# Matmuls of zeros in TensorE's idle time of the early plan, and accumulators at fixed places in PSUM, in an mLSTM layer followed by an ELU feed-forward

## The chip, the cores and the metric

One core of a Trainium2 chip. The metric is the device time of one execution in microseconds. TensorE (PE) has a clock with two levels, 1.2 and 2.4 GHz; the profile gives the granted level of a stretch as 0.50 or 1.00.

## The reference

For 4 batches, 8 heads, 768 steps and a head size of 40, a matrix memory is decayed, updated and read at every step; the result is gated, and the 3072 rows of 320 go through two weight matrices with an ELU between them, all in float32:

```python
m_new = max(f + m, i);  fs = exp(f + m - m_new);  is_ = exp(i - m_new)
C = fs * C + is_ * outer(v, k);   n = fs * n + is_ * k
y = sigmoid(o) * (C @ q) / max(|n . q|, 1)
h = x @ w_in                      # x: y as (3072, 320); w_in (320, 2048)
g = where(h > 0, h, exp(min(h, 0)) - 1)
out = g @ w_out                   # w_out (2048, 320)
```

## The kernel before

The sequence is cut into 6 chunks of 128 steps; with 4 batches that makes 24 tiles. `gate_chunk(c)` prepares the gates of a chunk: scans on VectorE (DVE), exponentials on ScalarE (ACT), and one TensorE transpose (line 467) whose result `iT` every tile of the chunk needs. `attention(n)` makes one tile: `products` (L555, scores of 8 heads), `values` (L563, `va`, from `iT`), `spread` (L581, TensorE copies a row of gates to all partitions; only in the first two chunks), `decays` (L595, a VectorE scan over it), the product of scores and decays (L609), `outputs` (L623 and L631), `update` (L644) and `gather` (a copy or an addition into `C`), `denominators` (L673), `result` (L687, `xf`), and `turn` (L704), three transposes; ScalarE (L707) and VectorE (L710) split the result into two float32r parts, `xh` and `xl`.

`conversion(i)` (L324 to L358) splits a piece of the weights into two float32r parts. It passes through ScalarE, VectorE, GpSimd (POOL), ScalarE and VectorE again. `ffn` runs over units: a unit is a block of 2 or 3 tiles and a range of the 16 slices of the hidden layer. For each slice there are 8 matmuls into `h` (L746), two ScalarE activations (L754, L757), a VectorE operation (L759), the split into `gh` (ScalarE, L762) and `gl` (L764), and 3 matmuls for each tile of the block into the tile's accumulator (L773). At the end of a unit each accumulator is copied to SBUF, by whichever of ScalarE and VectorE the plan picks (L232), or added to an earlier sum (L791), and stored.

The order is made by `Plan`: each operation is recorded with a cost for each engine that may run it, and `run` plays them against those costs, giving each free engine the ready operation of the best rank. Pools have a number of buffers (`room`); an operation waits until a buffer is free. The order that results is fixed for each engine, and engines execute it in order. Semaphores, and so waits, come from the tile framework, by which tile an instruction touches. Before, each accumulator is a tile of its own, `T("acc", (u, j), P, 512)`, from a pool of three in PSUM; for each of them the next user waits for the last reader.

Of the kernel before, what the change touches and what calls it, by code (L numbers as in the profile page):

```python
# [11 lines left out]
F32 = mybir.dt.float32  # L12
F32R = mybir.dt.float32r
BF16 = mybir.dt.bfloat16
# [6 lines left out]
P = 128  # L21
# [16 lines left out]
class Plan:  # L38
# [38 lines left out]
        self.ops.append(o)  # L77
        return o

    def run(self):  # L80
        for i, o in enumerate(self.ops):
            o.number = i
        for o in reversed(self.ops):
            own = min(o.engines.values())
            if o.nbytes:
                own += self.LAND + o.nbytes / self.RATE
            o.tail = own + max([0.0] + [a.tail for a in o.after if a.rank == o.rank])
        users = {}
        for o in self.ops:
            for k in o.touched:  # L90
                if k[0] in self.room:
                    users[k] = users.get(k, 0) + 1
        taken = {p: [] for p in self.room}
        given, free_at = set(), {}
        waits = {o: len(o.before) for o in self.ops}
        when = {o: 0.0 for o in self.ops}
        pending = [o for o in self.ops if not waits[o]]
        engines = {e: 0.0 for o in self.ops for e in o.engines}
        queue, port, t, order, events = 0.0, 0.0, 0.0, [], {0.0}

        def fits(o):
            new = {}
            for k in o.touched:
                if k[0] in self.room and k not in given:
                    new[k[0]] = new.get(k[0], 0) + 1
            for k in o.touched:
                if k[0] in self.in_turn and k not in given and k[1] != len(taken[k[0]]):
                    return False
            for p, count in new.items():
                for i in range(count):  # L110
                    j = len(taken[p]) + i - self.room[p]
                    if j >= 0 and free_at.get(taken[p][j] if j < len(taken[p]) else None, 1e9) > t:
                        return False
            return True

        while len(order) < len(self.ops):
            assert events, "nothing can go on"
            t = min(events)
            events.discard(t)
            again = True  # L120
            while again:
                again = False
                ready = sorted(
                    (o for o in pending if when[o] <= t), key=lambda o: (o.rank, -o.tail, o.number)
                )
                ahead = dict.fromkeys(engines, 0.0)
                ahead["port"] = 0.0

                def start(o, e):

                    x = max(engines[e], t) + ahead[e]
                    return max(x, max(port, t) + ahead["port"]) if e in o.port else x

                for o in ready:
                    if not fits(o):
                        continue
                    best = min(o.engines, key=lambda e: start(o, e) + o.engines[e])
                    if start(o, best) > t:
                        ahead[best] += o.engines[best]
                        if best in o.port:  # L140
                            ahead["port"] += o.engines[best]
                        continue

                    for k in sorted(o.touched, key=str):
                        if k[0] in self.room and k not in given:
                            given.add(k)
                            taken[k[0]].append(k)
                    end = t + o.engines[best]
                    engines[best] = end
                    if best in o.port:  # L150
                        port = end
                    events.add(end)
                    if o.nbytes:
                        queue = max(queue, end, self.BEGIN) + o.nbytes / self.RATE
                        end = queue + self.LAND
                        engines[best] = max(engines[best], queue - self.DEEP)
                        events.add(engines[best])
                    order.append((t, o.number, best, o))
                    pending.remove(o)
                    for a in o.after:  # L160
                        waits[a] -= 1
                        hop = 0.0 if best in a.engines and len(a.engines) == 1 else self.HOP
                        when[a] = max(when[a], end + hop)
                        if not waits[a]:
                            pending.append(a)
                            events.add(when[a])
                    for k in o.touched:
                        if k in users:
                            users[k] -= 1
                            free_at[k] = 1e9  # L170
                            self.last[k] = max(self.last.get(k, 0.0), end + self.HOP)
                            if not users[k]:
                                free_at[k] = self.last[k]
                                events.add(free_at[k])
                    again = True
                    break
        self.end = max(engines.values())
        self.order = order
        for _, _, e, o in order:
            o.fn(e)  # L180
# [3 lines left out]
def tile_mlstm_then_elu_ffn(  # L184
# [11 lines left out]
    nc = tc.nc  # L196
    PSUM = bass.MemoryType.PSUM
    B, NC, _, D, _, HH, L = qk.shape
    DM, DFF = w_in.shape[1], w_in.shape[0] * w_in.shape[2]
# [9 lines left out]
    SPLITS = [(0, 8), (1, 8), (2, 8), (0, 16)]  # L209
    W2N = 2  # L210

    SPREAD_BY_PE = 2
    TMAX = max(BLOCKS)
    WMAX = max(512, W2N * DM)
# [8 lines left out]
    room = dict(  # L223
        wide=3, narrow=2, gates=2, rest=1, qk=3, bb=3, vko=3, w=3, va=2, wl=2, dec=2, den=2, xf=2,
        x=3, ps_a=3, h=2, acc=3, e=2, gh=4, gl=4, os=3,
    )
    plan = Plan(room, ("qk", "bb", "e", "gh", "gl", "os"))
    op = plan.op
    eng = {"PE": nc.tensor, "DVE": nc.vector, "ACT": nc.scalar, "POOL": nc.gpsimd, "SP": nc.sync}

# [13 lines left out]
    const = ctx.enter_context(tc.tile_pool(name="const", bufs=1))  # L244
    pools = {}

    def pool(name, space=None):
        kw = dict(space=space) if space is not None else {}
        pools[name] = ctx.enter_context(tc.tile_pool(name=name, bufs=room[name], **kw))
# [5 lines left out]
    pools["rest"] = ctx.enter_context(tc.tile_pool(name="rest", bufs=1))  # L255
    pool("ps_a", PSUM)
    pool("h", PSUM)
    pool("acc", PSUM)
    tiles = {}

    def T(name, i, *shape, dt=F32, part=""):

        if (name, i, part) not in tiles:
            tiles[name, i, part] = pools[name].tile(list(shape), dt, name=name + part)
        return tiles[name, i, part]
# [13 lines left out]
    conv_of_2 = {}  # L279
    for f in range(NF):  # L280
        g, j = divmod(f, G)
# [432 lines left out]
    def ffn(u, kb, f0, f1):  # L714
        tl = blocks[kb]
        nt = len(tl)
# [4 lines left out]
            return T("x", kb, P, 3, TMAX * L, dt=F32R, part=part)[:, t, 0:N]  # L721

        def acc(j):
            return T("acc", (u, j), P, 512)[:, 0:DM]

        for f in range(f0, f1):
            g, j = divmod(f, G)
            fs = slice(j * P, (j + 1) * P)
            k = step[u, f]
# [38 lines left out]
            def second_layer(e, f=f, g=g, j=j, ff=ff):  # L768
# [7 lines left out]
                        )  # L776

            op({"PE": 3 * nt * 0.147}, second_layer,
               (KG, KL, ("conv", conv_of_2[f // W2N], 0)), tuple(("acc", (u, a)) for a in range(nt)) + (("turn", 2),))
        for a, n in enumerate(tl):  # L780
            c, b = divmod(n, B)

            def os(a=a):
                return T("os", osn[u, a], P, DM)

            KA, KOS = ("acc", (u, a)), ("os", osn[u, a])
            if f0 > 0:
                op({"SP": 0.06}, lambda e, os=os, n=n: nc.sync.dma_start(os(), sums[n]),
                   (("sum", n),), (KOS,), nbytes=P * DM * 4)
                op(two_ps(DM),  # L790
                   lambda e, os=os, a=a: nc.vector.tensor_add(os(), acc(a), os()),  # L791
                   (KA,), (KOS,))
            else:
                op({"ACT": 0.15 + 0.00088 * DM, "DVE": 0.1 + 0.001 * DM},
                   lambda e, os=os, a=a: copy(e, os(), acc(a)), (KA,), (KOS,))
            if f1 < NF:

                def keep(e, os=os, n=n):
                    sums[n] = dram.tile([P, DM], F32, name=f"sum{n}_{f1}")
                    nc.sync.dma_start(sums[n], os())  # L800

                op({"SP": 0.06}, keep, (KOS,), (("sum", n),), nbytes=P * DM * 4)
            else:
                op({"SP": 0.06},
                   lambda e, os=os, b=b, c=c: nc.sync.dma_start(
                       out[b * S + c * L : b * S + (c + 1) * L, :], os()),
                   (KOS,), (), nbytes=P * DM * 4)
# [16 lines left out]
    step, osn, begin, need = {}, {}, {}, {}  # L824
# [40 lines left out]
        conversion(i)  # L865
    for u, (kb, f0, f1) in enumerate(units):
        ffn(u, kb, f0, f1)
    plan.run()


_OUT = ((3072, 320), "float32")
# [31 lines left out]
```

## Time and profile before

| | |
|---|---|
| median of 3 runs | 495.1 us (493.95 to 495.77) |
| the profiled execution's own time | 494.69 us |
| its span, first to last instruction | 492.6 us |
| busy: PE, DVE, ACT, POOL | 93%, 74%, 59%, 24% |
| chain that ended last, by engine | PE 86%, DVE 11%, ACT 2% |

The span leaves out 2.1 us around the first and the last instruction. A run of matmuls overlaps: the time from one start to the next is shorter than the length of one, so a run of n takes less than n lengths. Rows of TensorE's weight loads (PEld) run beside its matmuls.

### The profile page before, as it was taken

Reading aid. Unit: us, or ns where it says so; the run is one execution under the profiler, and the core shown is the slowest. Engines: PE = TensorE matmul, PEld = TensorE weight load, DVE = VectorE, ACT = ScalarE, POOL = GpSimd, SP = SyncE. Lnnn points to the kernel's source line nnn. Section 1 sums busy time; section 2 is a strip of 40 time slices with the busy share of each in tenths; the row PEclk is TensorE's granted clock in tenths of the full one; section 3 lists DMA queues with packets and bytes.
Section 4 is the critical chain, followed back from the end, with each engine's and each line's share of the span. In section 5 each row is a group of like instructions: output and inputs, shape, how many; then the busy total and the mean of one; then the engine's idle time right before and its main releaser. Section 6 shows DMA issues by size and latency. Waiting matters only on the chain.

```text
span 492.6 us, 12520 instructions
## 1 busy us (share of the span) xinstructions
PE 456.1 (93%) x5006; PEld 432.6 (88%) x5006; DVE 362.2 (74%) x752; ACT 288.4 (59%) x681; POOL 117.6 (24%) x151
## 2 busy tenths in 40 slices
PE   2535889999999999999999999999999999999997
PEld 2334878999999999999989999999999999999996
DVE  8989898998787987965896478873678365546543
ACT  3555945779876564646456464475447544654664
POOL 2444484244231253121220101430012031000000
PEclk9999979999999999999999999999999999999999
DMA  7665544433325353421441034540333030100000
GB/s 266 176 208 166 167 136 138 134 110 127 106 82 154 100 164 110 154 84 42 133 145 43 28 110 127 153 124 1 111 111 109 1 97 1 43 1 1 28 1 27
DMA packets 39001, 49.51 MB, mean 101 GB/s; under 512 B 3072, under 2 KB 31648, under 8 KB 38944
## 3 DMA queue, kind: packets, MB, share of 16 engines
q1 hardware_dynamic: 38944, 48.72, 31.9%
q8 instruction: 39, 0.64, 0.5%
q14 instruction: 18, 0.15, 0.1%
HBM read 43.32 MB, written 5.39 MB: 99 GB/s over the span
## 4 chain that ended last, share of the span: by engine, by line
PE 86%; DVE 11%; ACT 2%; issue 1%; DVEq 0%; ACTq 0%
PE h L746 36%; PE acc L773 34%; PE ps_a L555 5%; PE ps_a L631 3%; PE ps_a L623 3%; DVE w L595 2%; PE ps_a L644 1%; PE ps_a L704 1%; DVE narrow L343 1%; DVE w L358 1%; DVE narrow L333 1%; DVE e L759 1%; DVE narrow L338 1%; PE h L581 1%; DVE w L609 1%
## 5 line engine op out<-in xcount | busy, mean ns | idle before, releaser
L746 PE MATMUL h<-xh,w 128*128 128x384 f32 (+1 forms) x720 | 179.6, 325 | 3.6 <-DVE w L595 2.2
L773 PE MATMUL acc<-w,gh 128*128 128x320 f32 x768 | 175.4, 315 | 1.5 <-DVE w L358 1.5
L773 PEld LDWEIGHTS acc<-w,gh 128*128 128x128 f32 x768 | 128.3, 189 | 3.9 <-DVE w L358 1.7
L746 PEld LDWEIGHTS h<-xh,w 128*128 128x128 f32 x720 | 126.1, 189 | 6.4 <-DVE w L595 2.6
L759 DVE SCALAR_TENSOR_TENSOR e<-e,h 128x384 f32<-128x384 f32 (+1 forms) x144 | 72.7, 505 | 72.6 <-ACT e L757 71.9
L754 ACT ACTIVATE e<-h 128x384 f32<-128x384 f32 (+1 forms) x144 | 65.4, 454 | 101.8 <-PE h L746 96.0
L773 PE MATMUL acc<-w,gl 128*128 128x320 f32 x384 | 119.3, 311 | 0.0
L746 PE MATMUL h<-xl,w 128*128 128x384 f32 (+1 forms) x432 | 113.0, 320 | 0.0
L762 ACT CAST gh<-e 128x384 fp32r<-128x384 f32 (+1 forms) x144 | 67.8, 472 | 34.9 <-DVE e L759 34.8
L764 DVE TENSOR_TENSOR gl<-e,gh 128x384 fp32r<-128x384 f32 (+1 forms) x118 | 64.1, 544 | 27.0 <-ACT gh L762 23.9
L746 PEld LDWEIGHTS h<-xl,w 128*128 128x128 f32 x432 | 77.1, 189 | 0.0
L773 PEld LDWEIGHTS acc<-w,gl 128*128 128x128 f32 x384 | 72.5, 189 | 0.8 <-DVE gl L764 0.6
L757 ACT ACTIVATE e<-e 128x384 f32<-128x384 f32 (+1 forms) x144 | 70.5, 490 | 3.8
L595 DVE TENSOR_TENSOR_SCAN w<-w,ident 128x512 f32<-128x512 f32 x32 | 40.0, 1249 | 5.6 <-DMA w<-f_d 5.4
L764 POOL TENSOR_TENSOR gl<-e,gh 128x384 fp32r<-128x384 f32 (+1 forms) x26 | 25.4, 978 | 63.2 <-ACT gh L762 59.0
L348 POOL TENSOR_TENSOR narrow<-narrow,wide 128x512 int32<-128x512 int32 (+1 forms) x18 | 27.4, 1523 | 41.9 <-DVE narrow L343 24.5
L570 ACT ACTIVATE vko<-vko 128x320 f32<-128x320 f32 x72 | 33.6, 467 | 2.7 <-DMA vko<-in_vko 1.9
L555 PE MATMUL ps_a<-qk 40*128 40x128 f32 x384 | 32.4, 316 | 0.0
L609 DVE TENSOR_TENSOR w<-ps_a,w 128x512 f32<-128x512 f32 x48 | 31.1, 679 | 1.3 <-PE ps_a L555 0.8
L555 PEld LDWEIGHTS ps_a<-qk 40*128 40x128 f32 x384 | 27.4, 216 | 4.4 <-issue 3.7
L655 POOL TENSOR_TENSOR C<-C,dec 40x164 f32<-40x164 f32 x28 | 16.1, 576 | 60.8 <-PE ps_a L623 59.8
L563 POOL TENSOR_TENSOR va<-vko,iT 128x320 f32<-128x320 f32 x15 | 14.1, 938 | 65.6 <-issue 33.4
(87 smaller groups left out, 419.8 us busy)
## 6 DMA issues: line engine op xcount, KB each, us to landing
vko<-in_vko SPq DMA_DIRECT2D x24, 480.0 KB
w<-f_d SPq DMA_DIRECT2D x32, 256.0 KB
qk<-in_qk SPq DMA_DIRECT2D x48, 160.0 KB
wide<-in_w_out SPq DMA_DIRECT2D x8, 640.0 KB
wide<-in_w_in SPq DMA_DIRECT2D x8, 512.0 KB
out<-os SPq DMA_DIRECT2D x24, 160.0 KB
bb<-b_d SPq DMA_DIRECT2D x40, 80.0 KB
sum<-os SPq DMA_DIRECT2D x8, 160.0 KB
```

Source lines behind the costliest of these rows:

```text
L348: lambda e: nc.gpsimd.tensor_add(narrow(), narrow(), words()[0]),
L555: nc.tensor.matmul(ps(two, P, HH, L)[:, j, :], kt[rows, j, :], qt[rows, j, :], start=True, stop=True,)
L570: lambda e, fn=fn, kw=kw: nc.scalar.activation(v3()[2], v3()[2], fn, **kw), (), (KS,))
L595: nc.vector.tensor_tensor_scan(a, f, ident4.rearrange("p h t -> p (h t)"), 0.0, op0=ALU.mult, op1=ALU.add)
L609: lambda e, half=half: nc.vector.tensor_mul(w(half), ps(half, P, HH, L), w(half)),
L746: nc.tensor.matmul(h(), a[g][:, fs], m, start=(i == 0), stop=(i == len(prods) - 1))
L754: op(act(N), lambda e, h=h, ff=ff: nc.scalar.activation(ff("e"), h(), AF.Relu, scale=-1.0), (KHP,), (KE,))
L757: lambda e, ff=ff: nc.scalar.activation(ff("e"), ff("e"), AF.Exp, scale=-1.0), (), (KE,))
L759: lambda e, h=h, ff=ff: nc.vector.scalar_tensor_tensor(out=ff("e"), in0=ff("e"), scalar=-1.0, in1=h(), op0=ALU.add, op1=ALU.max),
L762: op(act(N), lambda e, ff=ff: nc.scalar.copy(ff("gh", F32R), ff("e")), (KE,), (KG,))
L764: lambda e, ff=ff: eng[e].tensor_sub(ff("gl", F32R), ff("e"), ff("gh", F32R).bitcast(F32)),
L773: nc.tensor.matmul(acc(a), x[:, sl], bw[g][:, j, :], start=(f == f0 and i == 0), stop=(f == f1 - 1 and i == 2),)
```

## The change

`run` takes an operation `idle` and a time `until`. Whenever no operation can be started at a moment of the plan, and TensorE is free and the plan's clock is below `until` (60 us), it places one `idle`, `keep_warm`: four matmuls of a 128 by 128 bf16 tile of zeros by itself, planned at 0.24 us, which add zeros to columns 384 to 511 of the first accumulator's bank, which no accumulator uses. Two VectorE memsets ahead of everything else set the tile and these columns to zero. The plan places 163 of them (652 matmuls).

The three accumulators become parts of one tile, `accs`, and are given out in turn: accumulator `osn[u, j]` lies at place `osn[u, j] % 3`, and `acc` joins the list of pools that are taken in a fixed order. The test for that order now lets an operation take several places at once.

```diff
-    def run(self):
+    def run(self, idle=None, until=0.0):
...
-                if k[0] in self.in_turn and k not in given and k[1] != len(taken[k[0]]):
-                    return False
+                if k[0] in self.in_turn and k not in given:
+                    if not 0 <= k[1] - len(taken[k[0]]) < new[k[0]]:
+                        return False
...
+                else:
+                    if idle and engines["PE"] <= t < until:
+                        order.append((t, len(self.ops), "PE", idle))
+                        fillers += 1
+                        engines["PE"] = t + idle.engines["PE"]
+                        events.add(engines["PE"])
...
+    WARM = 60.0
...
-    plan = Plan(room, ("qk", "bb", "e", "gh", "gl", "os"))
+    plan = Plan(room, ("qk", "bb", "e", "gh", "gl", "os", "acc"))
...
-    pool("acc", PSUM)
+    ps_o = ctx.enter_context(tc.tile_pool(name="ps_o", bufs=1, space=PSUM))
+    accs = ps_o.tile([P, room["acc"], 512], F32, name="acc")
...
-            return T("acc", (u, j), P, 512)[:, 0:DM]
+            return accs[:, osn[u, j] % room["acc"], 0:DM]
...
-    plan.run()
+    warm = const.tile([P, P], BF16, name="warm")
+    nc.vector.memset(warm, 0.0)
+    nc.vector.memset(accs[:, 0, 512 - P :], 0.0)
+
+    def keep_warm(e):
+        for _ in range(4):
+            nc.tensor.matmul(
+                accs[:, 0, 512 - P :], warm, warm, start=False, stop=True, skip_group_check=True
+            )
+
+    plan.run(Op({"PE": 0.24}, keep_warm, (), 0, False), WARM)
```

Three places of the order follow (a line of the changed kernel is 12 above its fellow of before from L400 on; names in brackets are the semaphores that an instruction waits for: PE_49 TensorE's, DVE_49 VectorE's, Activation_49 ScalarE's, Pool_49 GpSimd's, DMAHW a transfer's).

The start of TensorE's queue, before, up to the second `spread` matmul:

```order
L897 UNCONDITIONAL_BRANCH [waits barrier_Pool_Activation_PE_DVE_SP_release]
L467 MATMUL ps_a<-ident,gatesi 128x32 [waits Activation_49,Pool_49]
L581 LDWEIGHTS sel [waits DVE_49]
L581 MATMUL h<-fgs,sel 128x128 [waits DVE_49]
L581 LDWEIGHTS sel
```

and with the change, with the pair `LDWEIGHTS warm`, `MATMUL acc<-warm` repeated 143 times where the first line of dots stands (36 fillers) and 11 times where the second does (3 fillers):

```order
L919 UNCONDITIONAL_BRANCH [waits barrier_Pool_Activation_PE_DVE_SP_release]
L886 LDWEIGHTS warm [waits DVE_49]
L886 MATMUL acc<-warm 128x128 [waits DVE_49]
...
L479 MATMUL ps_a<-ident,gatesi 128x32 [waits Activation_49,Pool_49]
L886 LDWEIGHTS warm
L886 MATMUL acc<-warm 128x128
...
```

The transpose of the gates, the first instruction of the queue before, now stands behind 36 fillers. Further on, in the same way: 1, 4, 5 and 13 fillers up to the first `turn`, 8 up to the second tile's `products`, 12, 4 and 2 around the next `spread`s, 32 and 14 before and after the `spread` that ran at 38 us, 1, 1, 1 and 11 up to the first slice of the first layer, 3 behind it, 10 between the third tile's `turn` and the second slice, and 2 ahead of the first second layer. None stands behind that. Apart from the fillers TensorE's order is the same.

VectorE's queue behind the denominators of the first tile (`-` before, `+` with the change; the same instructions on either side of them); the copy of `C` and the small copy of `xf` are now in ScalarE's queue, as is one copy of `wl` further on:

```order
 L232 COPY C_146<-ps_a 40x4x41 x2
 L683 TENSOR_TENSOR vko<-vko,den 128x320
 L687 TENSOR_TENSOR xf<-ps_a,vko 128x320
 L358 TENSOR_TENSOR w_119<-narrow,w_119 128x512
 L232 COPY xf<-xf 128x64
```

That piece is the queue of before; with the change its first and its last row are gone from it and the three between them follow each other.

VectorE's queue at the end of the unit that ends at 425 us in the trace, before; `os_5879` and `os_5883` are the first and the third accumulator's copy, the second's, `os_5881`, is ScalarE's and waits for PE_49 as well:

```order
L764 TENSOR_TENSOR gl_5868<-e_5849,gh_5866 128x256 [waits PE_49,Activation_49]
L232 COPY os_5879<-acc_5307 128x320 [waits DMAHW0_49,PE_49]
L232 COPY os_5883<-acc_5315 128x320 [waits DMAHW2_49,PE_49]
L759 SCALAR_TENSOR_TENSOR e_5896<-e_5896,h_5870 128x256 [waits DVE_49,Activation_49]
L764 TENSOR_TENSOR gl_5917<-e_5896,gh_5906 128x256 [waits Activation_49]
```

and with the change, where ScalarE's copy of the second accumulator is `L243 COPY os_6509<-acc_119 128x320 [waits DVE_49]`:

```order
L776 TENSOR_TENSOR gl_6496<-e_6477,gh_6494 128x256 [waits PE_49,Activation_49]
L243 COPY os_6507<-acc_119 128x320 [waits DMAHW0_49,PE_49]
L243 COPY os_6511<-acc_119 128x320 [waits DMAHW2_49,Activation_49]
L771 SCALAR_TENSOR_TENSOR e_6522<-e_6522,h_6498 128x256 [waits DVE_49,Activation_49]
L776 TENSOR_TENSOR gl_6543<-e_6522,gh_6532 128x256 [waits Activation_49]
```

Of the three copies the first waits for TensorE, the second for the first copy and the third for the second copy, since they now touch one tile; the first's wait is for the last matmul into any of the three places, where before each waited for the last into its own. The next unit's first matmul waits for the third copy. So it stands at every end of a unit whose copies go to both engines; copies or additions that all stand on one engine follow each other there in both kernels.

## Rows read from the trace of the kernel before

**Rows 1.** The page, the span in 40 equal slices of 12.3 us: tenths of busy time of VectorE, and the granted TensorE clock in tenths.

```profile
DVE  8989898998787987965896478873678365546543
PEclk9999979999999999999999999999999999999999
```

**Rows 2.** Busy time of each engine in stretches of the span. Columns: the stretch, its length, PE, PEld, DVE, ACT and POOL busy us (instructions), granted clock (1.00 is 2.4 GHz, 0.50 is 1.2 GHz), DMA share, GB/s.

```profile
0.00:10.00 10.00, 0.77 (x6) 0.77 (x7) 7.92 (x25) 3.24 (x7) 3.59 (x12) 1.00 0.70 234
10.00:20.00 10.00, 7.58 (x122) 6.17 (x122) 9.48 (x21) 5.36 (x11) 2.19 (x3) 1.00 0.62 199
20.00:30.00 10.00, 5.27 (x98) 4.50 (x96) 9.08 (x13) 6.27 (x13) 5.73 (x7) 1.00 0.73 228
30.00:40.00 10.00, 0.81 (x16) 0.38 (x8) 9.40 (x16) 4.35 (x10) 3.09 (x3) 1.00 0.62 205
40.00:47.00 7.00, 3.92 (x103) 3.26 (x103) 6.90 (x14) 4.79 (x11) 4.59 (x5) 1.00 0.52 165
67.80:74.60 6.80, 6.80 (x108) 5.98 (x106) 5.83 (x12) 3.46 (x9) 5.64 (x7) 0.50 0.69 208
300.00:400.00 100.00, 100.00 (x1065) 95.30 (x1064) 68.00 (x135) 54.60 (x124) 17.88 (x25) 1.00 0.28 85
```

**Rows 3.** The chain of waits of the first 100 us, in order of time: start us, length us, engine, tile, line, instructions. L581 is `spread` (128 columns of bf16 each), L555 `products`, L631 `outputs`, L746 the first layer, L773 the second, L704 the transposes.

```profile
10.53 2.06 PE ps_a L555 x16
...
26.88 2.07 PE ps_a L555 x16
28.95 1.29 PE ps_a L631 x64
...
47.05 2.07 PE h L746 x8
49.13 1.87 PE ps_a L555 x16
...
55.05 1.15 PE acc L773 x6
...
76.95 0.96 PE h L746 x8
77.91 0.33 PE ps_a L704 x3
...
96.26 0.38 PE h L581 x4
```

**Rows 4.** TensorE's instructions in order of time: start us, length us of a run of equal instructions, count, and in brackets the idle time before and what ended it. The second row is the end of one run of L581 (one of its instructions lasts 0.31 us).

```profile
8.14 0.28 PE L467 MATMUL ps_a<-ident,gatesi 32*128 32x32 f32 x1 [8.14 <-ACT gatesi L440]
...
9.89 0.63 PE L581 MATMUL h<-fgs,sel 96*128 96x128 bf16 x4
...
51.23 0.37 PE L746 MATMUL h<-xh,w 128*128 128x256 f32 x1
...
60.56 1.16 PE L555 MATMUL ps_a<-qk 40*128 40x128 f32 x16
...
66.71 0.38 PE L746 MATMUL h<-xh,w 128*128 128x256 f32 x1 [1.25 <-DVE e L759]
```

**Rows 5.** VectorE's instructions in order of time, same columns. L563 is `values`, L595 the scans, L609 the product with the scores, L343 and L358 the weight conversion, L673 `denominators`, L710 the lower part of x.

```profile
1.02 0.91 DVE L409 MEMSET qk<- 32x1024 f32 x1 [1.02 <-PEq L891]
...
9.49 0.49 DVE L563 TENSOR_TENSOR va<-vko,iT 128x320 f32<-128x320 f32 x1
...
15.88 0.61 DVE L232 COPY C<-ps_a 40x164 f32<-40x164 f32 x2
...
30.27 0.17 DVE L673 TENSOR_SCALAR denneg<-ps_a 128x8 f32<-128x8 f32 x1 [1.02 <-PE ps_a L631]
```

**Rows 6.** ScalarE's instructions in order of time, same columns: the first conversion copy (L354).

```profile
16.89 0.62 ACT L354 CAST w<-narrow 128x512 fp32r<-128x512 f32 x1 [3.05 <-POOL narrow L348]
```

**Rows 7.** All engines around three ends of a unit (the copies of the accumulators are `os<-acc`), same columns: at 116 us, at 138 us, at 425 us.

```profile
116.35 0.49 DVE L232 COPY os<-acc 128x320 f32<-128x320 f32 x1
116.42 0.79 ACT L232 COPY os<-acc 128x320 f32<-128x320 f32 x2
116.44 0.31 PE L773 MATMUL acc<-w,gl 128*128 128x320 f32 x1
...
118.00 0.46 PE L773 MATMUL acc<-w,gh 128*128 128x320 f32 x2
...
138.40 0.75 ACT L232 COPY os<-acc 128x320 f32<-128x320 f32 x2
...
139.03 0.43 ACT L757 ACTIVATE e<-e 128x256 f32<-128x256 f32 x1
...
424.87 1.03 DVE L232 COPY os<-acc 128x320 f32<-128x320 f32 x2
424.97 0.42 ACT L232 COPY os<-acc 128x320 f32<-128x320 f32 x1 [0.48 <-PE acc L773]
425.06 0.31 PE L773 MATMUL acc<-w,gl 128*128 128x320 f32 x1
...
426.16 0.46 PE L773 MATMUL acc<-w,gh 128*128 128x320 f32 x2
```

**Rows 8.** All engines at the end of the span, same columns: the last matmul of all and the last copy of an accumulator.

```profile
488.95 0.31 PE L773 MATMUL acc<-w,gl 128*128 128x320 f32 x1
489.30 0.42 ACT L232 COPY os<-acc 128x320 f32<-128x320 f32 x1 [1.41 <-PE acc L773]
```

More of the change, by code (lines that the diff above doesn't have):

```diff
@@ L114, in fits @@
             return True
-        while len(order) < len(self.ops):
+        fillers = 0
+        while len(order) - fillers < len(self.ops):
             assert events, "nothing can go on"
@@ L142, in run @@
                         continue
-                    for k in sorted(o.touched, key=str):
+                    for k in sorted(o.touched, key=lambda k: (k[0], len(str(k[1])), str(k[1]))):
                         if k[0] in self.room and k not in given:
@@ L778, in ffn @@
             op({"PE": 3 * nt * 0.147}, second_layer,
-               (KG, KL, ("conv", conv_of_2[f // W2N], 0)), tuple(("acc", (u, a)) for a in range(nt)) + (("turn", 2),))
+               (KG, KL, ("conv", conv_of_2[f // W2N], 0)), tuple(("acc", osn[u, a]) for a in range(nt)) + (("turn", 2),))
         for a, n in enumerate(tl):
@@ L784, in os @@
                 return T("os", osn[u, a], P, DM)
-            KA, KOS = ("acc", (u, a)), ("os", osn[u, a])
+            KA, KOS = ("acc", osn[u, a]), ("os", osn[u, a])
             if f0 > 0:
```

## The prediction

> **What bounds the kernel now.** I read the page's slices first. VectorE is busy in eight or nine tenths of nearly every slice up to 90 us and falls to five and less later [rows 1]. The table by stretches says the same with TensorE beside it: from 10 to 47 us VectorE works 34.9 of 37 us and TensorE 17.6, while from 300 to 400 us TensorE works all of the time [rows 2]. So there are two stages: up to about 65 us VectorE's fixed queue sets the pace and TensorE waits for it; behind that TensorE is the bound, and every us in which it stands still is a us of the end.
>
> Then TensorE's clock. The granted clock reads 1.00 in every stretch before 67 us [rows 2], but the durations speak against it: 16 matmuls of `products` take 2.06 us at 10 and at 27 us and 1.16 at 60 us; eight of the first layer take 2.07 at 47 us and 0.96 at 77 [rows 3, 4]. Matmuls of 128 bf16 columns follow each other at (0.63 - 0.31)/3 = 0.107 us at 10 us [rows 4], and four of them take 0.38 us at 96 us [rows 3], about half of that pace's. TensorE therefore ran at 1.2 GHz up to some point in the `products` of 49 us, which took 1.87 us in place of 2.06, about 50.7 us. It ran so again from 67.8 to 74.6 us, and there the granted clock says it too: 0.50 [rows 2]; ahead of the fall TensorE had waited, 1.25 us of it in one piece before 66.71 [rows 4]. The Trainium skill (TensorE: Matmul & The Clock Gate, "What's actually happening") says that the low clock is the default and activity releases it, and warns that such records can be unreliable; the matmul durations agree with the default, and the row of 1.00 doesn't. By that row alone the fillers would all run fast, and my sum below would end at about 497.6.
>
> **The change, part by part.** *The fillers, price.* At the high clock one filler (four matmuls) costs 4 x 0.055 = 0.22 us, at the low one 0.43. The plan counts 0.24.
>
> *The fillers, at the start.* VectorE now does two memsets first; 1024 elements took 0.91 us [rows 5], so these of 64 and 128 cost an estimated 0.3 us in all, on VectorE's queue from 1.02 us on, and TensorE starts at 1.3. The gates' transpose, which ran at 8.14 us [rows 4], stands behind 36 fillers. Even with the high clock from the first they end at 1.3 + 36 x 0.22 = 9.2, later than it was wanted. How long the low clock lasts isn't shown; the nearest rows are 3.65 us (work from 47.05 to the rise at 50.7 [rows 3]) and 6.8 us (67.8 to 74.6 [rows 2]). With their middle, 5.2, it is 12 slow fillers and 24 fast ones: 1.3 + 5.1 + 5.3 = 11.7 us; with the ends 11.0 and 12.7. VectorE's `va` needs that transpose through a ScalarE copy, some 0.5 us behind it: it goes from 9.49 [rows 5] to 12.2, **2.7 us late**, and VectorE's whole queue is behind it.
>
> *What gives that back.* VectorE's waits for TensorE on the way are few, so a fast TensorE returns little: 1.02 us before the denominators at 30.27 [rows 5], and 0.2 elsewhere. The copy of `C` that leaves its queue (0.61 us [rows 5]) returns nothing, for the conversion copy L358 behind it needs ScalarE's L354, which itself waited 3.05 us for GpSimd [rows 6], and that chain hangs on VectorE's earlier conversion step, late like the rest. So the first first-layer slice starts 2.7 - 1.2 = 1.5 us late, at 48.6. There TensorE is on the chain: that slice (0.96 now), three fillers (0.66), `products` (1.1) and the transposes (0.33) end at 51.7, against 51.2 before [rows 3, 4]. Now the plan has 10 fillers, 2.2 us, ahead of two slices that ran right there at 51.23. They end at 51.7 + 2.2 + 1.9 = 55.8, two more fillers follow, and the second layer starts at 56.3 where it started at 55.05 [rows 3]: 1.3 us late. No filler stands behind it; part of that is taken back in TensorE's gaps up to 65 us. I take **+1.0 us** for the early stage; with the clock's two ends, +0.2 to +1.8.
>
> *The clock after 60 us.* The idle time ahead of 66.71 us is VectorE's and has no filler in it. I take the fall at 67.8 as it was: **0**; if it doesn't come, TensorE, busy throughout those 6.8 us, needs 3.4 us less. That is a rival below.
>
> *Accumulators in one tile.* This is in the order, not in the plan: the copies at the end of a unit wait for the last matmul of the unit and for each other, and the next unit waits for the last copy. Before, they ran side by side: at 425 us VectorE's pair from 424.87 and ScalarE's from 424.97, and the next unit's second layer started at 426.16 [rows 7]. Now the chain starts when the last matmul ends, 425.06 + 0.31 = 425.37: 0.49 + 0.42 + 0.49 and three hand-overs of 0.04, so it ends at 426.9 and TensorE, with only one slice of the first layer between, stands still for **0.75 us**. At 116 us, where slices are longer, the chain of 0.42 + 0.49 + 0.42 runs from 116.75 to 118.2, against 118.00 [rows 7]: **0.25**. At the end of the kernel the copies were parallel too; VectorE's now starts at 489.30 and ScalarE's 0.53 us later than its 489.30 [rows 8]: **0.53**. At 138 us there is more TensorE work between, which covers the copies, but ScalarE's next activation stood right behind its second copy, at 139.03 [rows 7], and moves to about 140.1; what waits for its `gh` is at most 1.1 us late, at least nothing; the second layer follows closely, so **0.8**. Four other ends with mixed copies (263, 322, 375, 460 us) have two slices between: **0.2** in all, 0 to 1.0. Ends whose copies stand on one engine cost nothing. Sum **2.6**, between 1.6 and 3.7. Nothing gives it back, since TensorE has no idle time there [rows 2].
>
> **Sum.** The profiled execution took 494.69 us, 0.4 below the median of the runs. 494.7 + 1.0 + 2.6 = **498.3 us**; with the ends of both terms 496.5 to 500.2.
>
> **Rivals.** A. *The clock holds at 67.8 us.* With the fillers TensorE comes denser to that place, and where the fall lies in its gaps may shift. Then 498.3 - 3.4 = 494.9: no change. For it: the gap is short. Against it: VectorE makes it, and it is the same gap.
>
> B, the other side. *All of the low clock's cost was on the path.* The five cold pieces of the chain at 10.5, 26.9, 28.9, 47.05 and 49.1 us sum to 9.4 us [rows 3]; halved, 4.7 less. With the fall at 67.8 gone as well: 494.7 - 4.7 - 3.4 + 2.7 (the start) + 2.6 = 491.9, faster. It decides at the first layer: if that starts before 47 us, TensorE and not VectorE held the early stage. For it: the chain names these pieces. Against it: VectorE is busy 9.1 to 9.5 of 10 us beside them [rows 2].
>
> C. *Zeros don't raise the clock*, the change doesn't do what it says. Then 148 fillers up to the first layer cost 0.43 each, 63.6 us, and TensorE's own work of 18.4 us [rows 2] comes on top: the first layer starts at 83 us instead of 47, and the end is 494.7 + 36 + 2.6 = 533 us. No row shows TensorE on zeros. The Trainium skill (TensorE: Matmul & The Clock Gate, the note on the peak-current limiter) says that zero operands don't trip that other throttle; of the clock gate it says only that it watches how busy the engine is. No run here shows either; with it I leave C small.
>
> **How the numbers follow.** The forecast has a chance of 0.61, A 0.22, B 0.13, C 0.04. A measurement of this kernel can tell 0.5%, 2.5 us, from no change: below 492.6 or above 497.6. The forecast's case lies above 497.6 with 0.45 of its 0.61, C with all of its 0.04, A with 0.01: slower 0.50. B lies below 492.6 with 0.09, A with 0.01: faster 0.10. The rest is 0.40. The range reaches from A's lower part, 493.0, to the forecast's upper end, 500.4.
>
> **What would show it.** Right: the transpose L479 at 11 to 12.7 us and `va` right behind it; L567 at 1.16 us from 10 us on; the first L758 at 48 to 49 us, not before 47; ScalarE's and VectorE's copies of `acc` one behind the other, and TensorE idle 0.7 us ahead of L785 near 428 us. Wrong: the first L758 before 47 us, copies side by side, a granted clock of 1.00 from 60 to 80 us, or fillers at 0.107 us a matmul beyond 8 us.

## The result and the profile after

The changed kernel takes **498.51 us** (median of 20 runs, 495.12 to 500.10) against 494.98 of the kernel before (20 runs, 492.77 to 496.63): ratio 1.0056, 95% interval 1.0036 to 1.0076, so 0.6% slower. The execution whose profile follows took 500.03 us (span 498.1).

The runs fall into two groups by the mean granted clock that each of them records. In 7 of 20 it is 0.999, with a median of 495.48 us; in 11 it is 0.989 to 0.992, with a median of 499.29; two lie between (0.995 and 0.996: 496.15 and 497.22). The profiled execution, at 0.990, is of the long group.

First the page: the slices that answer to [rows 1], and two groups of matmuls (busy us, mean ns of one, idle time just before and its releaser).

```profile
DVE  5999997998878888875897378883768464446543
...
PEclk9999978999999999999999999999999999999999
...
L785 PE MATMUL acc<-w,gh 128*128 128x320 f32 x768 | 175.6, 315 | 0.8 <-DVE os L243 0.6
...
L886 PE MATMUL acc<-warm 128*128 128x128 bf16 x652 | 42.3, 227 | 1.2 <-DVE acc L882 1.2
```

VectorE's first slice has gone from 8 to 5: it now waits at the start. The fillers (L886, four matmuls each, 163 of them) are there, and second-layer matmuls wait for `os`, that is for a copy of an accumulator. The table by stretches, as in [rows 2]:

```profile
10.00:20.00 10.00, 10.00 (x230) 9.42 (x228) 7.11 (x13) 3.84 (x10) 2.20 (x3) 1.00 0.44 153
20.00:30.00 10.00, 9.59 (x161) 9.13 (x160) 9.86 (x15) 7.51 (x17) 5.61 (x7) 1.00 0.61 198
...
68.30:78.60 10.30, 10.01 (x122) 9.03 (x123) 7.52 (x15) 3.84 (x10) 6.74 (x9) 0.50 0.62 189
```

TensorE is now busy all of 10 to 20 us, and VectorE lost 2.4 us there (7.11 in place of 9.48). The stretch at 1.2 GHz behind 68 us is still there, and longer: 10.3 us in place of 6.8. Next TensorE in order of time, as in [rows 4]:

```profile
1.18 10.90 PE L886 MATMUL acc<-warm 128*128 128x128 bf16 x144 [1.18 <-DVE acc L882]
12.02 0.24 PE L479 MATMUL ps_a<-ident,gatesi 32*128 32x32 f32 x1
...
13.42 1.16 PE L567 MATMUL ps_a<-qk 40*128 40x128 f32 x16
...
48.64 0.36 PE L758 MATMUL h<-xh,w 128*128 128x256 f32 x1
...
51.92 2.40 PE L886 MATMUL acc<-warm 128*128 128x128 bf16 x40
54.13 0.37 PE L758 MATMUL h<-xh,w 128*128 128x256 f32 x1
...
56.56 0.54 PE L785 MATMUL acc<-w,gh 128*128 128x320 f32 x2
...
66.70 0.40 PE L593 MATMUL h<-fgs,sel 96*128 96x128 bf16 x4 [0.55 <-DVE w L607]
68.59 0.58 PE L758 MATMUL h<-xh,w 128*128 128x256 f32 x1 [1.49 <-DVE e L771]
...
71.04 2.08 PE L567 MATMUL ps_a<-qk 40*128 40x128 f32 x16
```

The gates' transpose stands behind 144 matmuls of zeros and ends at 12.26 us instead of 8.42. `products` take 1.16 us from 13.4 us on, in place of 2.06 at 10.53 before [rows 3]: zeros do raise the clock. The first first-layer slice starts at 48.64 us (47.05 before), the second layer at 56.56 (55.05 before). The idle time ahead of 68.59 us is the one that stood ahead of 66.71 before, and behind it `products` take 2.08 us again. VectorE's side, as in [rows 5]:

```profile
12.52 0.49 DVE L575 TENSOR_TENSOR va<-vko,iT 128x320 f32<-128x320 f32 x1 [2.90 <-ACT iT L243]
...
31.81 0.17 DVE L685 TENSOR_SCALAR denneg<-ps_a 128x8 f32<-128x8 f32 x1
```

`va` is 3.03 us late [rows 5]; at the denominators the lateness is 1.54, and VectorE no longer waits there. All engines at the end of a unit near 429 us and at the end of the span, as in [rows 7, 8]:

```profile
429.10 0.31 PE L785 MATMUL acc<-w,gl 128*128 128x320 f32 x1
...
429.45 0.49 DVE L243 COPY os<-acc 128x320 f32<-128x320 f32 x1 [0.46 <-PE acc L785]
...
429.97 0.43 ACT L243 COPY os<-acc 128x320 f32<-128x320 f32 x1 [1.45 <-DVE os L243]
430.43 0.49 DVE L243 COPY os<-acc 128x320 f32<-128x320 f32 x1 [0.49 <-ACT os L243]
...
430.98 0.56 PE L785 MATMUL acc<-w,gh 128*128 128x320 f32 x2 [0.62 <-DVE os L243]
...
494.07 0.31 PE L785 MATMUL acc<-w,gl 128*128 128x320 f32 x1
494.42 0.49 DVE L243 COPY os<-acc 128x320 f32<-128x320 f32 x1 [0.95 <-PE acc L785]
...
494.95 0.43 ACT L243 COPY os<-acc 128x320 f32<-128x320 f32 x1 [1.93 <-DVE os L243]
```

The copies form a chain: each waits for the one before it, though they read different accumulators, and TensorE waits 0.62 us for the last. (At the second end shown no unit follows.)

### The profile page after: what moved, and what is told of

The parts are those of the page before. It is cut to its first block, busy times and chain, and to the rows that moved or that the text cites. A ratio compares the mean times of both kernels' runs of the same rounds, so it can differ in the third digit from the quotient of the medians.

```text
span 498.1 us, 13825 instructions
## 1 busy us (share of the span) xinstructions
PE 487.4 (98%) x5658; PEld 465.2 (93%) x5658; DVE 362.2 (73%) x750; ACT 290.2 (58%) x685; POOL 116.6 (23%) x151
## 4 chain that ended last, share of the span: by engine, by line
PE 87%; DVE 8%; ACT 2%; DMA 1%; issue 1%; SPq 0%; DVEq 0%; ACTq 0%
PE h L758 35%; PE acc L785 33%; PE acc L886 5%; PE ps_a L567 4%; PE ps_a L643 3%; PE ps_a L635 3%; PE ps_a L656 1%; PE ps_a L716 1%; DMA qk<-in_qk 1%; DVE w L607 1%; DVE e L771 1%; DVE narrow L355 1%; DVE w L370 1%; ACT e L769 1%; DVE C L667 1%
## 5 line engine op out<-in xcount | busy, mean ns | idle before, releaser
L886 PE MATMUL acc<-warm 128*128 128x128 bf16 x652 | 42.3, 227 | 1.2 <-DVE acc L882 1.2
L886 PEld LDWEIGHTS <-warm 128*128 128x128 bf16 x652 | 39.7, 102 | 1.7 <-DVE warm L881 1.0
```

The costliest lines, as they stand in the source:

```text
L886: nc.tensor.matmul(accs[:, 0, 512 - P :], warm, warm, start=False, stop=True, skip_group_check=True)
```

## The experiments

Every kernel is the changed one with the edit shown, and each ratio is against runs of the kernel before on the same chip; those had medians of 494.94 to 495.42 us.

**Three accumulator tiles in place of one.**

```diff
-    accs = ps_o.tile([P, room["acc"], 512], F32, name="acc")
+    accs = [ps_o.tile([P, 512], F32, name=f"acc{j}") for j in range(room["acc"])]
...
-            return accs[:, osn[u, j] % room["acc"], 0:DM]
+            return accs[osn[u, j] % room["acc"]][:, 0:DM]
...
```

> Fillers as in the change, but the three places in PSUM are three tiles, so that copies of different accumulators no longer wait for each other. Theory (2.6 us of the loss lie in the chained copies): 2.5 us under the change, about 496.0 us, and at the ends of units ScalarE's and VectorE's copies side by side; what is left, +1.0, is the early stage. Rival 1 (all of the loss is the fillers' early stage and the clock's fall): as the change, 498.5. Rival 2 (all of it is the copies): 495.0.

495.93 us, ratio 1.0012 (0.9987 to 1.0038): 2.6 us less than with one tile, and no difference from before that these runs show. The same two places as above, all engines:

```profile
427.50 1.03 DVE L243 COPY os<-acc 128x320 f32<-128x320 f32 x2
...
427.59 0.43 ACT L243 COPY os<-acc 128x320 f32<-128x320 f32 x1 [0.47 <-PE acc L785]
...
427.69 0.31 PE L785 MATMUL acc<-w,gl 128*128 128x320 f32 x1
...
491.43 0.49 DVE L243 COPY os<-acc 128x320 f32<-128x320 f32 x1 [0.51 <-PE acc L785]
...
491.52 0.31 PE L785 MATMUL acc<-w,gl 128*128 128x320 f32 x1
491.87 0.43 ACT L243 COPY os<-acc 128x320 f32<-128x320 f32 x1 [1.41 <-PE acc L785]
```

The copies run side by side again, and start before the unit's last matmul.

What each end of a unit cost can be read from the two profiles, in which the low clock behind 68 us lasts equally long: the second layer's matmuls of the one were matched with those of the other by their order, and the lateness of the changed kernel was followed along them. It grows by 0.36 us behind the end at 116 us (times of the kernel before), 0.62 behind that at 138, 0.04 over the three at 263, 322 and 375, 0.90 behind that at 425 and 0.25 behind that at 460; the stretch from the last matmul to the end of the span is 0.38 longer. That is 2.55 us in all. Behind the end at 138 TensorE does not wait for a copy. ScalarE's next activation, which stands behind its second copy, starts at 143.61 us instead of 141.91, and 7 us after the copies TensorE waits for a late `gl`:

```profile
149.93 0.42 PE L785 MATMUL acc<-w,gl 128*128 128x320 f32 x1 [0.58 <-DVE gl L776]
```

That is a row of the changed kernel; with three tiles TensorE has no such wait there.

**One tile and no fillers**, the other half alone: `plan.run()` as before, without the memsets.

> No fillers and no memsets; only the accumulators as parts of one tile. Theory: the early stage and the clock as before, 2.6 us more at the ends of units: 497.6 us, with TensorE idle 0.7 us ahead of the second layer near 426 us. Rival 1 (copies are hidden): 495.0. Rival 2 (all of the loss is the copies): 498.5.

497.65 us, ratio 1.0047 (1.0025 to 1.0068), 2.7 more than before; TensorE waits 0.62 us for the last copy at 426.6 us. By the medians the chain of copies costs 2.6 to 2.7 us with and without fillers.

**Eighteen more fillers at the very start** (three tiles): `for _ in range(18): idle.fn("PE")` ahead of the order.

> Separate tiles and the change's fillers, and 18 more at the start, all of them ahead of the gates' transpose. Theory (what is ahead of the transpose delays va, and so VectorE's whole queue, one for one): va 18 x 0.22 = 4.0 us later than with separate tiles alone, the first scan at 17.0, the end 4.0 us later: 499.9. Rival (VectorE's idle time and TensorE's fast matmuls take most of a start delay back): under 498.

499.54 us, ratio 1.0104 (1.0082 to 1.0127): 3.6 more than the three tiles alone, 0.20 us a filler.

```profile
1.18 13.87 PE L898 MATMUL acc<-warm 128*128 128x128 bf16 x216 [1.18 <-DVE acc L894]
14.98 0.24 PE L491 MATMUL ps_a<-ident,gatesi 32*128 32x32 f32 x1
...
52.09 0.36 PE L770 MATMUL h<-xh,w 128*128 128x256 f32 x1
```

Against the three tiles alone the transpose moved by 3.24 us (from 11.74) and the first slice by 3.68 (from 48.41): nothing behind it takes the delay back.

**Eighteen fewer** (three tiles; fillers 19 to 36 left out when the order is issued, real work as it was):

```diff
+            if o is idle:
+                n += 1
+                if n - 1 in range(18, 36):
+                    continue
...
             o.fn(e)
```

> Separate tiles, the order of the change's own plan for everything that is real work, and 18 of the 36 fillers ahead of the gates' transpose left out. Theory (those 36 are too many, and the loss of the kernel with fillers at their true price came behind 65 us, from its other order and from two falls of the clock): the transpose on time, VectorE's scan of 63.8 us at 62.6 as there, 2.7 us ahead of separate tiles alone, the end 2.7 us under it: about 493.2 us. Rival (a VectorE that is early loses its lead again behind 65 us in any order): 496 to 498, no better than separate tiles alone.

492.76 us, ratio 0.9965 (0.9949 to 0.9981), 3.2 less than the three tiles alone.

```profile
1.18 5.91 PE L898 MATMUL acc<-warm 128*128 128x128 bf16 x72 [1.18 <-DVE acc L894]
8.29 0.22 PE L491 MATMUL ps_a<-ident,gatesi 32*128 32x32 f32 x1 [1.20 <-ACT gatesi L464]
...
54.46 0.54 PE L797 MATMUL acc<-w,gh 128*128 128x320 f32 x2
...
66.10 0.45 PE L770 MATMUL h<-xh,w 128*128 128x256 f32 x1 [1.25 <-DVE e L783]
...
66.30:69.70 3.40, 3.40 (x24) 3.11 (x25) 3.30 (x6) 1.58 (x5) 2.52 (x4) 0.50 0.59 154
```

The transpose waits for its input again, and the fillers before it lie in idle time. The last row, in the columns of [rows 2], is the low clock behind the wait at 66 us: 3.4 us long here.

**The plan given the price of the low clock** (three tiles; a filler counts 0.45 us before 6 us, and none is planned before 1.2 us):

```diff
...
-                        engines["PE"] = t + idle.engines["PE"]
+                        engines["PE"] = t + (idle.engines["PE"] if t > 6.0 else 0.45)
```

> Separate tiles, and the plan prices a filler as the chip does: none before 1.2 us, 0.45 us each up to 6 us of the plan, 0.24 behind it; 21 fillers and not 36 stand ahead of the gates' transpose. Theory: the transpose at about 8.6 us, va not late, VectorE's waits of 1.2 us and TensorE's slow pieces at 47 us returned: the first slice of the first layer at 46 us, the end 1 to 2 us under before, about 493.5. Rival (a fast TensorE returns nothing since VectorE sets the pace): 495.0, the first slice at 47.

A miss: 498.05 us, ratio 1.0064 (1.0038 to 1.0089). The start was as wanted: transpose at 8.30 us, first scan at 10.14, the first-layer slice at 46.2. But the plan now put TensorE's real work behind 60 us in another order, and the granted clock was 0.77 from 60 to 70 us and 0.72 from 70 to 80, with a second fall at 89 us. Which of these lost the lead isn't separated; the run before it, which changes the start alone, answers the question that this one was meant for.

**Fillers up to 80 us** (three tiles, `WARM = 80.0`).

> Separate tiles, fillers as in the change but up to 80 us of the plan, so also ahead of the place where the clock fell at 68 us. Theory: the clock holds at 2.4 GHz in every run, 3.4 us or more less than with the fall, and no two groups of run times: 493 us against 496 for separate tiles alone. Rival (the added fillers delay what stands behind them, as at 52 us): 496 to 498 with the clock held.

496.43 us, ratio 1.0037 (1.0016 to 1.0059). In nine of the twelve runs the clock held (mean 0.998 to 1.0); they took 495.4 to 496.9 us. The other three, at 0.995 to 0.997, took 498.5 to 499.0, so the clock seems to have fallen in them. Even where it held nothing was gained over before: TensorE's `64.51 3.08` below is 13 fillers in a row, and VectorE's next scan starts at 67.85 us, having waited 0.29 us for the spread behind them. That is the rival's outcome.

```profile
64.33 0.24 PE L479 MATMUL ps_a<-ident,gatesi 32*128 32x32 f32 x1
64.51 3.08 PE L886 MATMUL acc<-warm 128*128 128x128 bf16 x52
67.42 0.39 PE L593 MATMUL h<-fgs,sel 96*128 96x128 bf16 x4
```

**Half of the first 36, and seven fillers at 64 to 66 us**: two ahead of the first and five ahead of the second real step that the plan sets behind 67 us.

```diff
+        more = {1: 2, 2: 5}
...
+            elif e == "PE" and t > 67.0:
+                late += 1
+                for _ in range(more.get(late, 0)):
+                    idle.fn("PE")
```

> The kernel with half of the first 36, and 7 fillers (1.5 us) more in TensorE's idle time at 65 us: two ahead of the second spread there and five ahead of the slice of the first layer behind it, which waited 0.55 and 1.25 us. Theory: the clock holds at 68 us in every run and the fillers delay nothing, since TensorE is idle there: run times in one group, 3.4 us under the runs that fell, about 491 us in the median. Rival (7 fillers, as the 14 of the kernel up to 80 us, delay the slice more than the clock returns): 493 to 495 with the clock held.

493.03 us, ratio 0.9963 (0.9947 to 0.9980), in the rival's range and not at the theory's 491: the clock held in eight of nine runs (0.999 or 1.0; the ninth, at 0.995, took 494.90), and the median is that of the kernel without the seven. Three runs of that kernel, at 0.998, took 491.12 to 491.83; why the seven do not reach these times is not shown.

**The same with none of the first 36.**

> As the kernel with seven at 65 us, but with none of the 36 fillers ahead of the gates' transpose. Theory: the transpose and va as before, the clock low for the first products and up a few us later, since the fillers from 11 to 30 us leave TensorE little idle time; within 0.5 us of the kernel with 18, about 491. Rival (the high clock from 8 us on is worth the slow matmuls it replaces): 2 us more than that kernel.

493.40 us, ratio 0.9967 (0.9953 to 0.9982): within 0.5 us of the kernel with 18 of them, as expected, though both lie 2 us above the 491 that was expected.

**The seven alone**, none of the plan's fillers.

> Three accumulator tiles, none of the plan's fillers at all, only the seven fillers ahead of the two TensorE steps at 64 to 66 us. Before's own 495.0 has a low clock to 50 us and again for 6.8 us behind 67.8 in its profiled execution. If the fall of the clock at 68 us costs before its price of 3.4 us (6.8 us of a busy TensorE at half rate), these seven fillers alone give 491.6 to 492.5. If VectorE's queue sets the pace of 62 to 74 us whether the clock holds or not, as the run with seven fillers beside half of the first 36 suggests, it gives no more than 1 us: 494 to 495. If the warm start is what gained, it stays at 495.0. The second layer should start at 55.0, as before.

493.21 us, ratio 0.9960 (0.9941 to 0.9979), between the two first outcomes: a gain of 1.8 us, half of 3.4, from seven fillers. The twelve runs lie close together, at 492.47 to 493.61. The table by stretches, then TensorE:

```profile
20.00:30.00 10.00, 5.28 (x98) 4.50 (x96) 8.93 (x13) 6.84 (x15) 5.68 (x7) 1.00 0.71 230
...
50.00:60.00 10.00, 10.00 (x129) 8.94 (x128) 9.32 (x24) 8.83 (x23) 5.00 (x6) 0.74 0.46 145
60.00:70.00 10.00, 8.90 (x100) 7.59 (x98) 9.64 (x22) 5.36 (x17) 6.95 (x9) 1.00 0.39 111
```

```profile
65.21 1.28 PE L897 MATMUL acc<-warm 128*128 128x128 bf16 x20
66.62 0.38 PE L769 MATMUL h<-xh,w 128*128 128x256 f32 x1
...
68.06 1.16 PE L578 MATMUL ps_a<-qk 40*128 40x128 f32 x16
70.07 0.79 PE L646 MATMUL ps_a<-C,bb 104*64 104x82 f32 x16 [0.85 <-DVE bb L597]
```

No filler stands ahead of 64 us, and TensorE is as busy from 20 to 30 us as before; in this execution its clock was low again from 48 to 55 us (0.74 in the second row). At 68 us it is fast, and then it waits 0.85 us for VectorE, which is busy 9.64 of the 10 us ahead: of the rest of the 3.4 us that much is seen here.

**Half of the first 36, without the last 12 fillers** (the 10 ahead of the two slices and the 2 ahead of the second layer): `or n > total - 12` in the condition above.

> The half of the first 36 (492.76) with the last 12 of the plan's fillers left out as well: the 10 ahead of the two slices at 50 us and the 2 ahead of the second layer. The prediction counted them at 2.2 and 0.44 us on TensorE's queue. If they cost what they delay, the two slices start at 49.8 instead of 52.0 and the second layer at 54.05 (when VectorE's conversion of w ends) instead of 54.46: 0.4 us less at least, 492.0 to 492.4, and a transfer of e that is 2 us earlier. If TensorE's idle time of some 2 us ahead of the second layer lets the clock fall there, the low clock returns around 55 us for some us and the time is 493.5 to 495.

493.35 us, ratio 0.9962 (0.9939 to 0.9984). The place was right, the time wasn't:

```profile
53.23 0.56 PE L798 MATMUL acc<-w,gh 128*128 128x320 f32 x2 [1.35 <-DVE w L383]
...
65.27 0.58 PE L771 MATMUL h<-xh,w 128*128 128x256 f32 x1 [1.49 <-DVE e L784]
...
67.73 2.08 PE L580 MATMUL ps_a<-qk 40*128 40x128 f32 x16
```

The second layer starts 7.57 us behind the first slice (45.66 in this profile) in place of 7.92 (46.54): the 12 cost 0.35 us there. The rest of the 1.23 us by which it is earlier was there already at the first slice, with the same instructions ahead: a wait of VectorE's conversion for ScalarE, 0.94 us at 18.4 us in the other profile, is missing in this one. The clock did not fall near 55 us, as the rival had it, but at the old place, and the lead was lost there: the low clock lasts 10.2 us in this profile and 3.4 in the one with the 12. Mean clocks of 0.988 to 0.998 say that its length differs among the runs of this one kernel, and the two medians don't tell the kernels apart. In the two runs whose mean clock was 0.997 and 0.998 the time was 492.04 and 490.61.

**Without the last 12, and the seven at 64 to 66 us.**

> Half of the first 36, none of the last 12, and the seven fillers at 64 to 66 us: the early lead of 1.2 us (second layer at 53.23 in place of 54.46) with a clock that holds. If the lead is lost only to the longer low clock (64.6 to 72 us in that profile), this gives the time of the two of its runs in which the clock held, 490.6 to 492.0, plus at most 0.5 us for the fillers: 491.5. If VectorE's queue of 62 to 74 us sets the pace whatever the clock does, it stays at 493.0 to 493.3, the time of the seven fillers alone and of seven beside half of the 36.

491.80 us, ratio 0.9934 (0.9911 to 0.9957), nearer to the first theory's 491.5 than to 493. The clock held in eight of nine runs; the ninth, at 0.997, took 494.11. It is 1.2 less than seven beside the late 12, with intervals that overlap; of that the two profiles show 0.5 at VectorE's scan of 95 us (94.71 and 95.22), and spans 0.8 apart.

**The same with five**, `{2: 5}`.

> The same with five fillers ahead of the second step only (none ahead of the spread at 63.4 us). If the clock holds with five too, within 0.4 us of the run with seven, or that much faster, since two fillers of 0.2 us no longer stand in the queue; if the two ahead of the first step are needed to hold it, the runs split into two groups again, and the median is 493 or more.

491.40 us, ratio 0.9923 (0.9896 to 0.9949), the shortest of all: 138 fillers instead of 163, and accumulators in tiles of their own. Against the seven the intervals overlap.

```profile
53.74 0.56 PE L798 MATMUL acc<-w,gh 128*128 128x320 f32 x2 [1.35 <-DVE w L383]
...
64.13 1.28 PE L899 MATMUL acc<-warm 128*128 128x128 bf16 x20
65.78 0.39 PE L771 MATMUL h<-xh,w 128*128 128x256 f32 x1 [0.36 <-DVE e L784]
...
67.22 1.16 PE L580 MATMUL ps_a<-qk 40*128 40x128 f32 x16
68.82 0.79 PE L648 MATMUL ps_a<-C,bb 104*64 104x82 f32 x16 [0.44 <-DVE bb L599]
```

## Why the prediction was right, and where it was not

The median came out 0.2 us from the forecast. The chain of copies is right in mechanism and in size. The other two terms, +1.0 for the early stage and 0 for the clock, are right only as a sum: the step on the clock failed, and that the sum fits is luck.

*Price and start: right.* A filler was put at 0.22 us; 18 of them cost 3.6 us more and 3.2 us less. The start was put at 11.7 us for the transpose and 12.2 for `va`; the rows show 12.02 and 12.52. 144 matmuls in 10.90 us are some 56 at 0.107 us and the rest at 0.055, so 14 slow fillers, where 12 were counted.

*What gives it back: right.* Of 3.03 us the way to the first layer returned 1.4, mostly ahead of the denominators, as predicted; the first slice starts at 48.64 us (48.6), the second layer at 56.56 (56.3).

*The clock behind 60 us, 0: this step failed.* I took the fall as a fixed feature of the kernel. It comes in most runs and is missing in others, and where it comes it is 10.3 us long in the profile after, against 6.8. Rival A, with 494.9 us, is what the runs at 0.999 show (495.48). The kernel before has such groups too, which I had not looked for: of its 20 runs five took 492.8 to 494.0 us, eleven 494.8 to 495.8 and four 496.4 to 496.6. So its median lies in the middle group, that of the profile with 6.8 us of low clock, and the median after lies in the group of the profile with 10.3.

The price of 3.4 us for 6.8 us was wrong as well. With nothing else changed in the early stage, keeping the clock gained 1.8 us, the distance from the middle group of before to its fastest: the seven fillers alone put all their runs there. In the batches that list the clock of the kernel before, its runs at 0.963 to 0.965 have a median of 493.45 us and those at 0.954 one of 496.44, so 3.0 us for an estimated 10 us of low clock (0.010 x 495, twice); the profiled run of one tile without fillers has such a clock, 0.964, and shows no low clock from 56 us to 490. After, it is 3.8 us for 10.2. Half of the low stretch would be 5: part of what TensorE loses there is hidden, and in the run with seven fillers alone VectorE's queue is seen right behind.

*The early stage, +1.0: not shown at that size.* Three tiles against before give +1.0 us in the medians, but this is the term with the clock's behaviour in it. The profiles show 1.5 at the second layer and 1.9 at 66 us [rows 4]. Where groups of like clock are compared, less of it is left at the end: the five runs of three tiles at 0.997 to 1.0 have a median of 493.59 us, 0.1 above the 493.45 of before; the six with the long fall (496.53 to 497.80) one of 497.1, 0.6 above 496.44. By this reading the early stage cost some 0.1 to 0.6 us and the longer falls the rest of the 1.0. It rests on grouping runs by their mean clock, not on a run that holds the clock in both kernels.

*Accumulators in one tile, 2.6: right.* 2.6 by the three tiles, 2.7 by the one tile without fillers, 2.55 by the two profiles. TensorE's idle time at 431 us is 0.62 us (0.75), ScalarE's last copy starts 0.53 us behind VectorE's (0.53). End by end the profiles show 0.36 at 116 us (0.25 forecast), 0.62 at 138 (0.8), 0.90 at 425 (0.75), 0.29 at the four others (0.2) and 0.38 at the last (0.53).

*Rival B, TensorE holds the early stage: refuted in its strong form.* The first slice starts at 48.64 us, not before 47. Seven fillers alone, with none ahead of 64 us, give 493.21 us; the warm start added to them gives 493.03 with the late 12 and 491.80 without. So the warm start is worth 0.2 to 1.4 us here, by medians whose intervals overlap, not the 4.7 of that rival. In the profiles VectorE's scan of 95 us stands at 95.80, 95.22 and 94.71 in the three, 0.6 and 1.1 earlier than with the seven alone.

*Rival C: refuted* by `products` at 1.16 us from 13.4 us on.

*Slips in the working.* The parts of the 2.6 add up to 2.5, the later end of the start is 12.5 and not 12.7, and the range goes to 500.4 where the sum's end is 500.2. None of them matters.

So the change loses 2.6 us to the shared tile, some 3 us to 18 fillers too many at the start and by the profiles 0.4 to 0.5 to the 12 at 50 us (no medians show it), and it places none where the clock falls. The best kernel, 0.8% under the one before, mends these four.

## What to carry to other kernels

A filler on an in-order queue is an instruction like any other: where it exceeds the true idle time, the work behind it is late by its whole length, so its count is to be set by when the next real input arrives, with the low clock's price at the start. Here a low clock cost time only where TensorE was what was waited for; look for the short wait ahead of the fall and fill that, before warming stretches that another engine paces. Parts of one tile are not independent buffers: look at the waits of their readers before merging them. And where a kernel's runs fall into groups, compare group with group before two medians are subtracted: a median that moves from one group to the next looks like an effect of the edit.

## What the runs showed of the hardware

- Matmuls of zeros raise the clock to 2.4 GHz: after 5.7 us of them in the profile after, the granted-clock records show the high level from 6.9 us on. The Trainium skill (TensorE: Matmul & The Clock Gate, "What's actually happening") says that activity releases the throttle and that the moment varies from run to run; these traces agree: with the same first instructions the fillers' pace went from 0.107 to 0.056 us a matmul at 6.9 us (after), 6.3 (three tiles), 4.9 (18 fewer) and 4.7 (18 more). They add that the operands may be zero.
- After the same wait for VectorE at 65 to 68 us the stretch at 1.2 GHz lasted 10.3 us (after), 6.8 (before) and 3.4 (18 fewer fillers), and in 7 of 20 runs of the changed kernel the mean clock of 0.999 leaves room for about 1 us of it (0.001 x 495 us, twice, since the low clock is half): runs of the same program lie 3.8 us apart with that (499.29 and 495.48). What decides it from run to run stays open.
- Five fillers, 20 matmuls of 1.28 us in all, ahead of one step kept the clock in each of six runs (0.999 or 1.0). Seven, two of them ahead of an earlier step, did so in eight of nine runs of each of two kernels.
